# Gated layer and experts issued in a written order, low weight parts stored once and read back, logits spread over the next unit

## The chip, the cores and the metric

One Trainium2 chip, one of its cores. The metric is device time in microseconds (us) of one execution of the whole program; the kernel before has a median of 1438.2 us over three runs.

## What is computed

Three layers in one launch, all in float32. Attention with heads mixed before and after the softmax (4 batches, 12 heads, 448 positions, 64 per head) gives `x` of 1792 tokens by 768. Then a gated layer, then a layer of eight experts of which each token takes one:

```python
g = x @ w_gate                                  # 768 -> 1536
x = (g * (1.0 / (1.0 + np.exp(-g))) * (x @ w_val)) @ w_out
logits = x @ w_gate2                            # 768 -> 8
expert_idx = np.argmax(logits, axis=1)
gate_w = probs[np.arange(N), expert_idx]        # softmax of the logits
out[mask] = gate_w[mask, None] * (np.maximum(x[mask] @ w1[e], 0.0) @ w2[e])
```

## The kernel before

**Precision.** A matmul of the two layers runs as three matmuls (`mm3`, L485 to L488): every operand is split in a high part, a rounded copy, and a low part, the rest. The three products are high by high (L486), low weight by high (L487) and high weight by low (L488). So every weight tile is loaded as float32 (`wraw`, L471, 768 KB), copied on ScalarE into its high part (`whi`, L474) and subtracted into its low part (`wlo`, L476), on GpSimd for most tiles and on VectorE for those in `LOW_W`. Tiles are counted through: 0 to 17 are the gated layer's 18 tiles for the first unit, 18 to 71 the same 18 tiles three times more, 72 to 135 the experts'. In tiles 18 to 71 all low parts are made on GpSimd.

**Gated layer.** The tokens go in four units of 448. A unit has two stages. In the first, twelve tiles `ft`: 18 matmuls into the PSUM tile `pg` and 18 into `pv`; then ScalarE takes the exponential of `pg` (L618), VectorE adds 1 (L619), takes the reciprocal (L620), and multiplies by `pg` (L621) and by `pv` (L622); ScalarE and GpSimd split the product into `hhi` (L625) and `hlo` (L626). In the second, six tiles `c` of 36 matmuls over all twelve `hhi`/`hlo`; ScalarE copies each result to `x2T` (L656). The PSUM pool of these matmuls has five buffers, the pool of split weights four for each part, that of raw weights three.

**Rows, logits, routing.** After a unit, `rows` (L513) transposes `x2T` to token rows on TensorE (L520), copies them out of PSUM on VectorE and ScalarE (L522) and stores them (L524). `logits` (L526) then makes 32 dot products of rows with the experts' gate vectors on VectorE (L532, output `junk`), two to a tile of the next unit's first stage (`LGS`), and `route` (L537) picks the expert, counts each token's place in it with small matmuls (L552 to L567) and scatters token numbers and gates to a table (L584). The last unit makes half of each dot product on VectorE (L653) and the other half as matmuls (L640); the first expert's tokens are fetched (L601) by places taken from PSUM.

**Experts.** For each: 18 small transposes of fetched rows (L686), 144 + 144 matmuls of 264 columns, rectified and split on ScalarE and VectorE (L738, L739), and results transposed back (L702), scaled by the gate (L707, L709) and scattered (L711).

**Order.** Attention issues in a written order: inside `tc.manual_schedule` each engine takes its instructions as the program lists them, waits included. `feed_forward` has no such region before: a planner with its own cost estimates orders each engine's instructions, and `next_w` only says that loads and splits are traced up to three tiles ahead (`AHEAD`). Loads and stores go through SP's queue in the order in which SP gets to them; the planner places some of the gated layer's first instructions among attention's last ones.

Of the kernel before, what the change touches and what calls it, by code (L numbers as in the profile page):

```python
# [11 lines left out]
F32 = mybir.dt.float32  # L12
# [11 lines left out]
U = 448  # L24
# [20 lines left out]
LGS = [2] * 12 + [4, 4]  # L45
AHEAD = 3
# [369 lines left out]
def feed_forward(tc, xT, wf, wg, wt, w1, w2, cs, out, x2, tab, keep):  # L416
    nc = tc.nc
    V = nc.vector
    with ExitStack() as ctx:
# [3 lines left out]
        pm, pt, pr = P("pmm", 5, "p"), P("ptp", 2, "p"), P("prt", 1, "p")  # L423
        CS, NB = keep
        nc.sync.dma_start(out=CS, in_=cs)
        ID = CS[:, :128]
        IE = CS[:112, 352:384].rearrange("p (j e) -> p j e", e=NE)
        TH = CS[:112, 416:512].rearrange("p (e i) -> p e i", i=OVB)
        UO = cst.tile([112, 224], BF16, name="UO")
        V.tensor_copy(UO, CS[:112, 128:352])  # L430
        UT, ON = UO[:, :112], UO[:, 112:]
        ONF = CS[:112, 240:352]
        WG = cst.tile([128, 6, NE], F32, name="WG")
        nc.sync.dma_start(out=WG, in_=wg)
        WT = cst.tile([112, NE, DM], F32, name="WT")
        pf = cst.tile([128, NE * STR // 128, 2], I32, name="pf")
        nc.gpsimd.memset(pf[:, :, 0:1], NT)
        nc.gpsimd.memset(pf[:, :, 1:2], 0)
        nc.sync.dma_start(out=tab.rearrange("(p n) t -> p n t", p=128), in_=pf)
        zr = cst.tile([128, DM // 128], F32, name="zr")  # L440
        nc.gpsimd.memset(zr, 0.0)
        nc.sync.dma_start(out=x2[NT].rearrange("(p n) -> p n", p=128), in_=zr)
        ti = cst.tile([112, 4], I32, name="ti")
        nc.gpsimd.iota(ti, pattern=[[112, 4]], base=0, channel_multiplier=1)
        tf = cst.tile([112, 4], F32, name="tf")
        V.tensor_copy(tf, ti)
        tk = []
        for u in range(4):
            tk.append(cst.tile([112, 4], F16, name=f"tk{u}"))
            V.tensor_scalar(out=tk[u], in0=tf, scalar1=float(u * U - NT), scalar2=None, op0=ALU.add)  # L450
        iot = cst.tile([112, CAP], F16, name="iot")
        nc.gpsimd.iota(iot, pattern=[[1, CAP]], base=0, channel_multiplier=0, allow_small_or_imprecise_dtypes=True)
        first = cst.tile([TS, 3], F32, name="first")
        V.memset(first, float(NT))
        TB0 = cst.tile([TS, 3], I32, name="TB0")
        RS = cst.tile([112, NE], F32, name="RS")
        V.tensor_copy(RS, CS[:112, 384:392])

# [5 lines left out]
        ready, last, at = {}, {}, {"load": 0, "use": 0}  # L464

        def fill(n):
            while at["load"] <= min(n, len(src) - 1):
                k = at["load"]
                at["load"] += 1
                r = raw.tile([128, 12, 128], F32, name="wraw")  # L470
                last["w"] = nc.sync.dma_start(out=r, in_=src[k])  # L471
                a = wh.tile([128, 12, 128], F32R, name="whi")
                b = wh.tile([128, 12, 128], F32R, name="wlo")
                nc.scalar.copy(a, r)  # L474
                eng = nc.vector if k in LOW_W else nc.gpsimd
                eng.tensor_tensor(out=b, in0=r, in1=a.bitcast(F32), op=ALU.subtract)  # L476
                ready[k] = (a, b)

        def next_w():
# [10 lines left out]
        def order(inst, earlier):  # L490
            tc.add_manual_dep(from_inst=inst.ins, to_name=earlier.ins.name, info=mybir.DependencyInfo(mybir.DependencyClass.NoSync, mybir.DependencyReason.SCHED_ONLY))

        def apart(group, inst):
            tc.declare_no_dep(inst.ins, group=group, reason="every token has its own row")
            tc.add_to_no_dep_group(group, inst.ins)

        XS, routed = {}, []

        def load_x(u):
            XS[u] = []  # L500
            for c in range(6):
                r = xr.tile([128, U], F32, name="xraw")
                nc.sync.dma_start(out=r, in_=xT[:, c, u * U:u * U + U])
                a = xp.tile([128, U], F32R, name="xhi")
                b = xp.tile([128, U], F32R, name="xlo")
                nc.scalar.copy(a, r)
                nc.gpsimd.tensor_tensor(out=b, in0=r, in1=a.bitcast(F32), op=ALU.subtract)  # L507
                XS[u].append((a, b))
# [4 lines left out]
        def rows(u, x2T, row, halves):  # L513
            for j in range(4):
                if 0 in halves:
                    row.append(ro.tile([112, DM], F32, name="row"))
                for hf in halves:
                    t = pt.tile([128, 3, 128], F32, name="tp")
                    for i in range(3):
                        nc.tensor.transpose(t[:112, i, :], x2T[3 * hf + i][:, 112 * j:112 * j + 112], ID)  # L520
                    copy = nc.scalar.copy if hf else V.tensor_copy
                    copy(row[j][:, 384 * hf:384 * hf + 384], t[:112].rearrange("p i c -> p (i c)"))  # L522
                lo, hi = 384 * halves[0], 384 * halves[-1] + 384
                nc.sync.dma_start(out=x2[u * U + 112 * j:u * U + 112 * j + 112, lo:hi], in_=row[j][:, lo:hi])  # L524

        def logits(u, row):  # L526
            lg = T("lgs")
            done = 0
            for n in LGS:
                for j, e in [divmod(i, NE) for i in range(done, done + n)]:  # L530
                    jk = sm.tile([112, DM], F32, name="junk", bufs=1)
                    V.tensor_tensor_reduce(out=jk, in0=row[j], in1=WT[:, e, :], scale=1.0, scalar=0.0, op0=ALU.mult, op1=ALU.add, accum_out=lg[:, j, e:e + 1])  # L532
                done += n
                yield
            yield from route(u, lg)

        def route(u, lg):  # L537
# [23 lines left out]
            fi = pr.tile([112, 4, NE], F32, name="rt").rearrange("p j e -> p (j e)")[:TS, :3]  # L561
            eqs = [sm.tile([112, CAP], F16, name="at", bufs=4) for j in range(4)]
            for j in range(4):
                V.tensor_scalar(out=eqs[j], in0=iot, scalar1=sf[:, j, :], scalar2=None, op0=ALU.is_equal)
            for t in range(3):
                for j in range(4):
                    nc.tensor.matmul(fi[:, t:t + 1], eqs[j][:, t * TS:t * TS + TS], tk[u][:, j:j + 1], start=(j == 0), stop=(j == 3))  # L567
            V.tensor_tensor(out=TB0 if u == 3 else first, in0=fi, in1=first, op=ALU.add)
            if u == 3:
                fetch(0)  # L570
# [3 lines left out]
            nc.scalar.activation(ex, sh, AF.Exp)  # L574
# [3 lines left out]
            si = T("si", (112, 4), I32)  # L578
            V.tensor_copy(si, sf[:, :, 0])
            en = T("en", (112, 4, 2), I32)  # L580
            V.reciprocal(out=en[:, :, 1:2].bitcast(F32), in_=sx)
            V.tensor_scalar(out=en[:, :, 0], in0=tf, scalar1=float(u * U), scalar2=None, op0=ALU.add)
            for j in range(4):
                sc = nc.gpsimd.indirect_dma_start(out=tab, out_offset=bass.IndirectOffsetOnAxis(ap=si[:, j:j + 1], axis=0), in_=en[:, j, :], in_offset=None)  # L584
                apart("tab", sc)
                if u == 3:
                    order(sc, last["gather"])
                routed.append(sc)
            nr = T("nr", (112, NE, 1))
            V.tensor_reduce(out=nr, in_=oh.rearrange("p j e -> p e j"), axis=AX.X, op=ALU.add)  # L590
            V.tensor_tensor(out=RS, in0=RS, in1=nr[:, :, 0], op=ALU.add)

        TB = cst.tile([TS, NE, 3, 2], I32, name="TB")
        XE, RG = {}, {}

        def fetch(e):
            RG[e] = []
            for t in range(3):
                r = ro.tile([112, DM], F32, name="row")
                ap = TB[:, e, t, 0:1] if e else TB0[:, t:t + 1]  # L600
                last["gather"] = nc.gpsimd.indirect_dma_start(out=r[:TS, :], out_offset=None, in_=x2, in_offset=bass.IndirectOffsetOnAxis(ap=ap, axis=0))  # L601
                RG[e].append(r)


        fill(0)
        load_x(0)
        later = iter(())
        for u in range(4):
            hs = []
            for ft in range(12):  # L610
                w = next_w()
                pg = pm.tile([128, 512], F32, name="mm")
                pv = pm.tile([128, 512], F32, name="mm")
                for ps, o in ((pg, 0), (pv, 6)):
                    for c in range(6):
                        mm3(ps[:, :U], w, o + c, XS[u][c], c == 0, c == 5)
# [227 lines left out]
```

## Time and profile before

| | |
|---|---|
| three runs | 1437.43, 1438.2, 1438.92 us |
| profiled execution | 1438.62 us; span from first to last instruction 1436.8 us |
| mean granted TensorE clock | 0.978 of full speed |
| busy | PE 94%, PEld 82%, DVE 61%, ACT 46%, POOL 58% of the span |
| attention | to about 501 us |
| gated layer, units 0 to 3 | 501 to 637.6, to 787.3, to 937.5, to 1095.2 us |
| between gated layer and experts | 1095.2 to 1112.3 us |
| experts and end | 1112.3 to 1436.8 us |

PE is TensorE's matmuls, PEld its weight loads, DVE is VectorE, ACT ScalarE, POOL GpSimd, SP the engine that issues loads and stores. A unit's end is taken as the start of its last copy to `x2T`. Matmuls are pipelined: one of 448 columns lasts 0.36 us in the trace, and the next begins 0.20 us after it, so the number of matmuls in a stretch tells more than their busy time. The arrow in a row names what ended an idle time.

### The profile page before, as it was taken

To read this page: it belongs to the slowest core of one execution; us is meant where nothing else is said; L and a number is where in the kernel's file an instruction comes from. 1 tells how busy PE (TensorE), PEld (TensorE's weight loads), DVE (VectorE), ACT (ScalarE), POOL (GpSimd) and SP (SyncE) were. 2 spreads that over 40 slices of the span, in tenths; PEclk is the share of its full clock that TensorE was granted. 3 is DMA by queue.
4 is the path that set the end of the run, shared out by engine and by line. 5 is a ranking of instruction groups with operands and counts; after the bars stand their busy time and mean duration, and the time that the engine had idled before them with its cause. 6 is when DMAs were issued, how large, how long until landed. Compare 5 with 4: busy or idle time off the path is not lost.

```text
span 1436.8 us, 24827 instructions
## 1 busy us (share of the span) xinstructions
PE 1349.2 (94%) x9100; PEld 1174.4 (82%) x9100; DVE 874.8 (61%) x1691; ACT 661.8 (46%) x1261; POOL 835.0 (58%) x603
## 2 busy tenths in 40 slices
PE   8999999998999999999999998999986999999995
PEld 3677777776777789989889887988875999999995
DVE  3677777767767778429960998089946333333330
ACT  4675776767666533422232233232321445454551
POOL 4575566556644554735575467646643566666751
PEclk9999999999999999999999999999997999999998
DMA  7887887788786765432243323242333566666650
GB/s 244 244 256 236 232 260 242 224 260 251 223 246 208 231 206 168 139 126 98 91 134 123 127 89 110 98 143 88 110 107 108 142 221 197 216 196 209 198 174 21
DMA packets 106833, 251.23 MB, mean 175 GB/s; under 512 B 28189, under 2 KB 71293, under 8 KB 106591
## 3 DMA queue, kind: packets, MB, share of 16 engines
q1 hardware_dynamic: 102351, 237.54, 52.7%
q0 software_dynamic: 4352, 12.02, 3.0%
q8 instruction: 74, 1.21, 0.4%
q14 instruction: 56, 0.46, 0.1%
HBM read 180.00 MB, written 31.79 MB: 147 GB/s over the span
## 4 chain that ended last, share of the span: by engine, by line
PE 63%; DVE 20%; issue 6%; DMA 5%; ACT 3%; POOL 1%; SPq 1%; POOLq 0%; ACTq 0%; DVEq 0%
PE mm L488 12%; PE mm L486 12%; PE mm L487 12%; PE pso L275 8%; PE psm L247 7%; DVE e L620 7%; DVE junk L532 6%; PE psv L303 5%; PE psq L234 4%; DMA qraw<-in_qt 2%; DVE e L619 2%; DVE e L622 1%; DVE e L621 1%; PE tp L702 1%; DMA xm<-S 1%
## 5 line engine op out<-in xcount | busy, mean ns | idle before, releaser
L476 POOL TENSOR_TENSOR wlo<-wraw,whi 128x1536 fp32r<-128x1536 f32 x108 | 383.1, 3547 | 200.9 <-ACT whi L474 180.1
L486 PE MATMUL mm<-xhi,whi 128*128 128x448 f32 (+1 forms) x960 | 325.9, 340 | 11.3 <-DVE e L621 9.4
L488 PE MATMUL mm<-xlo,whi 128*128 128x448 f32 (+1 forms) x960 | 322.1, 336 | 1.4 <-POOL xlo L507 1.4
L487 PE MATMUL mm<-xhi,wlo 128*128 128x448 f32 (+1 forms) x960 | 322.0, 335 | 0.0
L474 ACT CAST whi<-wraw 128x1536 fp32r<-128x1536 f32 x136 | 200.9, 1477 | 68.1 <-PE mm L488 50.2
L486 PE MATMUL mm<-hhi,whi 128*128 128x264 f32 (+1 forms) x672 | 221.5, 330 | 7.6 <-ACT hhi L625 7.6
L488 PE MATMUL mm<-hlo,whi 128*128 128x264 f32 (+1 forms) x672 | 218.2, 325 | 1.8 <-POOL hlo L626 1.8
L487 PE MATMUL mm<-hhi,wlo 128*128 128x264 f32 (+1 forms) x672 | 217.4, 324 | 0.0
L275 PEld LDWEIGHTS pso<-kk,e 120*112 120x112 f32 x1440 | 170.5, 176 | 46.6 <-POOL kk L267 11.9
L486 PEld LDWEIGHTS mm<-xhi,whi 128*128 128x128 f32 x960 | 181.9, 190 | 24.5 <-DVE e L621 13.2
L275 PE MATMUL pso<-kk,e 120*112 120x120 f32 x1440 | 179.9, 268 | 13.6 <-ACT AT L283 7.0
L488 PEld LDWEIGHTS mm<-xlo,whi 128*128 128x128 f32 x960 | 181.7, 189 | 11.5 <-POOL xlo L507 2.1
L267 POOL TENSOR_SCALAR kk<-K,r 120x120 f32<-120x120 f32 x180 | 108.2, 602 | 140.9 <-DVE r L264 112.3
L487 PEld LDWEIGHTS mm<-xhi,wlo 128*128 128x128 f32 x960 | 182.3, 190 | 9.3 <-issue 0.2
L247 PE MATMUL psm<-xm,K 120*120 120x448 f32 x360 | 169.4, 553 | 5.8 <-DMA xm<-S 5.8
L255 ACT ACTIVATE e<-psm,nm 120x448 f32<-120x448 f32 x180 | 115.4, 641 | 98.3 <-DVE r L264 96.6
L620 DVE RECIPROCAL e<-e 128x448 f32<-128x448 f32 x48 | 141.5, 2947 | 0.7
L486 PEld LDWEIGHTS mm<-hhi,whi 128*128 128x128 f32 x672 | 128.6, 191 | 13.5 <-ACT hhi L625 8.7
L532 DVE CUSTOM_DVE_ANT_0 junk<-row,WT 112x768 f32<-112x768 f32 x96 | 135.0, 1407 | 0.9 <-ACT row L522 0.7
L488 PEld LDWEIGHTS mm<-hlo,whi 128*128 128x128 f32 x672 | 128.5, 191 | 8.3 <-POOL hlo L626 3.4
L487 PEld LDWEIGHTS mm<-hhi,wlo 128*128 128x128 f32 x672 | 128.8, 192 | 4.8
L626 POOL TENSOR_TENSOR hlo<-e,hhi 128x448 fp32r<-128x448 f32 x48 | 66.4, 1384 | 107.7 <-ACT hhi L625 107.7
(125 smaller groups left out, 2004.5 us busy)
## 6 DMA issues: line engine op xcount, KB each, us to landing
wraw<-wf SPq DMA_DIRECT2D x72, 768.0 KB
wraw<-in_w SPq DMA_DIRECT2D x64, 768.0 KB
xm<-S SPq DMA_DIRECT2D x360, 105.0 KB
f<-in_wx SPq DMA_DIRECT2D x72, 384.0 KB
wf<-cva SPq DMA_DIRECT2D x72, 192.0 KB
qraw<-in_qt SPq DMA_DIRECT2D x56, 180.0 KB
kraw<-in_kt SPq DMA_DIRECT2D x18, 448.0 KB
vt<-in_vt SPq DMA_DIRECT2D x16, 336.0 KB
```

Source lines behind the costliest of these rows:

```text
L247: nc.tensor.matmul(ps[:, :S], K1, XS.pop(n), start=True, stop=True)
L255: nc.scalar.activation(e, ps[:, :S], AF.Exp, bias=nm, scale=1.0, accum_out=su)
L267: nc.gpsimd.tensor_scalar(out=kk, in0=K2, scalar1=r2, scalar2=1.0, op0=ALU.mult, op1=ALU.mult)
L275: nc.tensor.matmul(po[:, c, :120], e[:, 112 * c:112 * c + 112], kk, start=True, stop=True)
L303: nc.tensor.matmul(pa[64 * s:64 * s + 64, j % 3, :n], VT[b][c][:, g * 64:g * 64 + 64], ATS[t][:, c, g, :n], start=(c == 0), stop=(c == 3))
L474: nc.scalar.copy(a, r)
L476: eng.tensor_tensor(out=b, in0=r, in1=a.bitcast(F32), op=ALU.subtract)
L486: nc.tensor.matmul(ps, w[0][:, j, :], x[0], start=first, stop=False)
L487: nc.tensor.matmul(ps, w[1][:, j, :], x[0], start=False, stop=False)
L488: nc.tensor.matmul(ps, w[0][:, j, :], x[1], start=False, stop=last)
L532: V.tensor_tensor_reduce(out=jk, in0=row[j], in1=WT[:, e, :], scale=1.0, scalar=0.0, op0=ALU.mult, op1=ALU.add, accum_out=lg[:, j, e:e + 1])
L620: V.reciprocal(out=e, in_=e)
```

## The change

- The whole of `feed_forward` becomes a written order on all five engines. Loads run to tile i+4 and splits to tile i+2 when tile i is taken (`take`).
- Tiles 0 to 17: the low part, once made, is stored to a DRAM tensor `wl` (`keep_low`, 18 stores of 768 KB). Tiles 18 to 71: the low part is loaded from `wl` by SP and not computed.
- The addition of 1 goes from DVE to ACT, as an activation with a bias.
- Rows of unit u are transposed, taken (both halves on ACT) and stored in the first four tiles of unit u+1; the 32 logits follow, none in tile 0, two in tiles 1 to 11, then 3, 3, 2, 2 in the second stage; `route` runs in its fourth to sixth tile.
- In the second stage the first two tiles `c` run eleven of their twelve steps, then both last ones. The next unit's `x` is split one chunk to a tile.
- The last unit's logits are all matmuls (six chunks in place of three), its first row halves are transposed in the second stage; around the routing stand ten extra matmuls (`warm`) whose results nobody reads.
- `gather(0)` stands ahead of the rest of `route`, whose table scatters follow it; a one-element memset goes to POOL with each scatter. The constants are made in tiles 1 and 4 of unit 0.

```diff
-LGS = [2] * 12 + [4, 4]
-AHEAD = 3
+LGS = [0] + [2] * 11 + [3, 3, 2, 2]
...
+        ctx.enter_context(tc.manual_schedule(engines=ORDERED))
...
+        def split(to):
+            while at["split"] <= min(to, len(src) - 1):
+                k = at["split"]
+                at["split"] += 1
+                r = rawt.pop(k)
                 a = wh.tile([128, 12, 128], F32R, name="whi")
                 b = wh.tile([128, 12, 128], F32R, name="wlo")
+                A.copy(a, r)
+                if 18 <= k < 72:
+                    nc.sync.dma_start(out=b.bitcast(F32), in_=wl[k % 18])
+                else:
+                    (V if k in LOW_W else G).tensor_tensor(out=b, in0=r, in1=a.bitcast(F32), op=ALU.subtract)
+                    if k < 18:
+                        kept.append((k, b))
                 ready[k] = (a, b)
...
+        def take():
             i = at["use"]
             at["use"] += 1
-            fill(i + AHEAD)
+            keep_low()
+            load(i + 3)
+            split(i + 2)
+            load(i + 4)
             return ready.pop(i)
...
+                if u > 0 and 1 <= ft <= 4:
+                    put_row(u - 1, ft - 1)
...
+                    if u > 0 and ft < 4:
+                        turn_row(u - 1, ft, o // 6)
                 e = ew.tile([128, U], F32, name="e")
-                nc.scalar.activation(e, pg[:, :U], AF.Exp, scale=-1.0)
-                V.tensor_scalar(out=e, in0=e, scalar1=1.0, scalar2=None, op0=ALU.add)
+                A.activation(e, pg[:, :U], AF.Exp, scale=-1.0)
+                A.activation(e, e, AF.Copy, bias=1.0)
                 V.reciprocal(out=e, in_=e)
...
+                if u > 0:
+                    for n in range(sum(LGS[:ft]), sum(LGS[:ft + 1])):
+                        logit(u - 1, n)
...
+            begin(0)
+            second(0, range(11))
+            beside(0)
+            begin(1)
+            second(1, range(11))
+            second(0, (11,))
+            end(0)
+            second(1, (11,))
+            end(1)
...
+        go = route(3)
+        warm(1)
+        chunk_logits(5)
+        next(go)
...
+        warm(2)
+        next(go)
+        fetch(0)
+        warm(6)
+        for _ in gather(0):
+            pass
+        for _ in go:
+            pass
```

## Rows read from the trace of the kernel before

**Rows 1.** Page, part 4: the chain that ended last, share of the span by engine
```profile
PE 63%; DVE 20%; issue 6%; DMA 5%; ACT 3%; POOL 1%; SPq 1%; POOLq 0%; ACTq 0%; DVEq 0%
```

**Rows 2.** Stretches: length, busy of PE, PEld, DVE, ACT, POOL, clock, DMA share, GB/s
```profile
501.00:637.60 136.60, 133.71 (x652) 122.74 (x649) 77.79 (x64) 47.67 (x56) 75.85 (x40) 0.99 0.50 160
637.60:787.30 149.70, 140.95 (x692) 126.99 (x691) 104.74 (x136) 46.28 (x59) 91.03 (x40) 0.98 0.35 114
...
937.50:1095.20 157.70, 145.28 (x713) 129.60 (x711) 128.32 (x201) 43.02 (x53) 81.42 (x33) 0.97 0.32 108
1095.20:1112.30 17.10, 6.76 (x53) 5.36 (x51) 7.94 (x29) 3.40 (x6) 9.30 (x7) 0.63 0.47 134
...
1150.00:1190.00 40.00, 40.00 (x340) 40.00 (x339) 14.24 (x21) 20.09 (x32) 26.56 (x15) 1.00 0.68 226
```

**Rows 3.** Stretches of 40 us in the first stages of units 0 and 1, same columns
```profile
560.00:600.00 40.00, 40.00 (x199) 37.09 (x198) 29.73 (x22) 15.40 (x20) 24.29 (x13) 1.00 0.35 112
...
660.00:700.00 40.00, 40.00 (x195) 36.32 (x195) 40.00 (x46) 11.83 (x14) 24.86 (x10) 1.00 0.26 89
```

**Rows 4.** Timeline of DVE, one tile of unit 1: start us, us, instruction
```profile
667.08 0.61 DVE L622 TENSOR_TENSOR e<-e,mm 128x448 f32<-128x448 f32 x1
...
668.80 2.94 DVE L620 RECIPROCAL e<-e 128x448 f32<-128x448 f32 x1
671.66 2.49 DVE L532 CUSTOM_DVE_ANT_0 junk<-row,WT 112x768 f32<-112x768 f32 x1
...
674.08 0.61 DVE L621 TENSOR_TENSOR e<-e,mm 128x448 f32<-128x448 f32 x1
674.61 0.94 DVE L532 CUSTOM_DVE_ANT_0 junk<-row,WT 112x768 f32<-112x768 f32 x1
...
675.49 0.61 DVE L622 TENSOR_TENSOR e<-e,mm 128x448 f32<-128x448 f32 x1
```

**Rows 5.** Timeline of POOL, the same tile
```profile
668.37 1.51 POOL L626 TENSOR_TENSOR hlo<-e,hhi 128x448 fp32r<-128x448 f32 x1 [3.45 <-ACT hhi L625]
669.84 3.49 POOL L476 TENSOR_TENSOR wlo<-wraw,whi 128x1536 fp32r<-128x1536 f32 x1
```

**Rows 6.** Waits of PE, 637 to 790 us: us in total, times, longest
```profile
PE mm L486 <- ACT hhi L625: 2.5, 1, 2.5
```

**Rows 7.** Groups of instructions, 560 to 1437 us: busy us, mean ns | idle before, releaser
```profile
L474 ACT CAST whi<-wraw 128x1536 fp32r<-128x1536 f32 x125 | 184.6, 1477 | 46.1 <-PE mm L488 34.6 <-issue 11.5
...
L619 DVE TENSOR_SCALAR e<-e 128x448 f32<-128x448 f32 x41 | 30.5, 745 | 13.5 <-ACT e L618 13.5
...
L625 ACT CAST hhi<-e 128x448 fp32r<-128x448 f32 x42 | 23.8, 568 | 162.6 <-DVE e L622 162.6
...
L618 ACT ACTIVATE e<-mm 128x448 f32<-128x448 f32 x41 | 22.3, 544 | 24.8 <-PE mm L488 22.7 <-POOL hlo L626 2.2
...
L567 PE MATMUL rt<-tk,at 112*88 112x1 f16 x48 | 4.5, 195 | 4.9 <-DVE at L564 4.9
...
L640 PE MATMUL mm<-WG,x2T 128*112 128x8 f32 x24 | 2.7, 237 | 0.0
```

**Rows 8.** Timeline of PE, unit 3: six transposes and the matmul behind them
```profile
1064.63 0.82 PE L520 MATMUL tp<-CS,x2T 128*112 128x128 f32 x6
1065.21 0.45 PE L486 MATMUL mm<-hhi,whi 128*128 128x448 f32 x1
```

**Rows 9.** Timeline of SP, from attention to the gated layer
```profile
486.86 0.43 SPq L471 DMA_DIRECT2D wraw<-wf  x1
...
504.25 0.56 SPq L312 DMA_DIRECT2D xT<-X  x1
```

**Rows 10.** Timeline of DVE, routing of the last unit
```profile
1097.77 2.55 DVE L543 TENSOR_TENSOR eq<-lgs,mx 112x32 f32<-112x32 f32 x1
```

**Rows 11.** DMA view, 520 to 1060 us: packets, MB, rate; the queue's share of 16 engines
```profile
DMA packets 14189, 64.12 MB, mean 119 GB/s; under 512 B 1824, under 2 KB 4128, under 8 KB 14048
...
q1 hardware_dynamic: 13904, 63.71, 35.7%
```

More of the change, by code (lines that the diff above doesn't have):

```diff
@@ L499, in load_x @@
[L499 to L508, printed above, removed]
+        XR, XS = {}, {}
@@ new lines, in load_x, with split_x @@
+        def load_x(u, c):
+            XR[u, c] = xr.tile([128, U], F32, name="xraw")
+            nc.sync.dma_start(out=XR[u, c], in_=xT[:, c, u * U:u * U + U])
+        def split_x(u, c):
+            r = XR.pop((u, c))
+            a = xp.tile([128, U], F32R, name="xhi")
+            b = xp.tile([128, U], F32R, name="xlo")
+            A.copy(a, r)
+            G.tensor_tensor(out=b, in0=r, in1=a.bitcast(F32), op=ALU.subtract)
+            XS.setdefault(u, []).append((a, b))
+        load(0)
@@ new lines, in feed_forward @@
+        for c in range(2):
+            load_x(0, c)
+        load(1)
+        split(0)
+        for c in range(6):
+            split_x(0, c)
+            if c < 4:
+                load_x(0, c + 2)
+        load(2)
+        split(1)
+        load(3)
+        WT = cst.tile([112, NE, DM], F32, name="WT")
+        WG = cst.tile([128, 6, NE], F32, name="WG")
+        UO = cst.tile([112, 224], BF16, name="UO")
+        pf = cst.tile([128, NE * STR // 128, 2], I32, name="pf")
+        ti = cst.tile([112, 4], I32, name="ti")
@@ new lines, in feed_forward @@
+        tf = cst.tile([112, 4], F32, name="tf")
+        tk = [cst.tile([112, 4], F16, name=f"tk{u}") for u in range(4)]
+        iot = cst.tile([112, CAP], F16, name="iot")
+        TB0 = cst.tile([TS, 3], I32, name="TB0")
+        first0 = cst.tile([TS, 3], F32, name="first")
+        gap = cst.tile([1, 1], F32, name="gap")
+        RS = cst.tile([112, NE], F32, name="RS")
+        ID = CS[:, :128]
+        IE = CS[:112, 352:384].rearrange("p (j e) -> p j e", e=NE)
+        TH = CS[:112, 416:512].rearrange("p (e i) -> p e i", i=OVB)
@@ L526, in logits @@
[L526 to L535, printed above, removed]
@@ L537, in route, with turn_row, take_row @@
-        def route(u, lg):
+        X2T, ROW, HALF, LG, routed, late = {}, {}, {}, {}, [], []
+        def turn_row(u, j, hf):
+            t = HALF[u, j, hf] = pt.tile([128, 3, 128], F32, name="tp")
+            for i in range(3):
+                nc.tensor.transpose(t[:112, i, :], X2T[u][3 * hf + i][:, 112 * j:112 * j + 112], ID)
+        def take_row(u, j, hf, eng=None):
+            if (u, j) not in ROW:
+                ROW[u, j] = ro.tile([112, DM], F32, name="row")
+            (eng or A.copy)(ROW[u, j][:, 384 * hf:384 * hf + 384], HALF.pop((u, j, hf))[:112].rearrange("p i c -> p (i c)"))
@@ new lines, in put_row, with logit, chunk_logits @@
+        def put_row(u, j, lo=0, hi=DM):
+            nc.sync.dma_start(out=x2[u * U + 112 * j:u * U + 112 * j + 112, lo:hi], in_=ROW[u, j][:, lo:hi])
+        def logit(u, n):
+            if n == 0:
+                LG[u] = T("lgs")
+            j, e = divmod(n, NE)
+            jk = sm.tile([112, DM], F32, name="junk", bufs=1)
+            V.tensor_tensor_reduce(out=jk, in0=ROW[u, j], in1=WT[:, e, :], scale=1.0, scalar=0.0, op0=ALU.mult, op1=ALU.add, accum_out=LG[u][:, j, e:e + 1])
+        def chunk_logits(c):
+            for j in range(4):
+                nc.tensor.matmul(LG[3][:, j, :], X2T[3][c][:, 112 * j:112 * j + 112], WG[:, c, :], start=(c == 0 and j == 0), stop=(c == 5 and j == 3))
@@ L674, in feed_forward @@
-        for t in range(3):
-            ld = nc.sync.dma_start(out=TB[:, :, t, :], in_=tab.rearrange("(e s) t -> s e t", e=NE)[t * TS:t * TS + TS])
-            for sc in routed:
-                tc.add_manual_dep(from_inst=ld.ins, to_name=sc.ins.name, info=mybir.DependencyInfo(mybir.DependencyClass.Sync, mybir.DependencyReason.DATA))
-        RT = cst.tile([112, NE, DM], F32, name="WT")
-        at["row"] = 0
         def gather(e):
@@ new lines, in feed_forward @@
+        go = route(3)
+        warm(1)
+        chunk_logits(5)
+        next(go)
+        for j in (0, 1):
+            turn_row(3, j, 1)
+        for j in (0, 1):
+            take_row(3, j, 1)
+            put_row(3, j, 384, DM)
+        warm(1)
+        next(go)
+        for j in (2, 3):
+            turn_row(3, j, 1)
+        for j in (2, 3):
+            take_row(3, j, 1)
+            put_row(3, j, 384, DM)
+        warm(2)
+        next(go)
+        fetch(0)
+        warm(6)
+        for _ in gather(0):
+            pass
@@ L694, in put @@
+        for _ in go:
+            pass
+        for t in range(3):
+            ld = nc.sync.dma_start(out=TB[:, :, t, :], in_=tab.rearrange("(e s) t -> s e t", e=NE)[t * TS:t * TS + TS])
+            for sc in routed:
+                tc.add_manual_dep(from_inst=ld.ins, to_name=sc.ins.name, info=mybir.DependencyInfo(mybir.DependencyClass.Sync, mybir.DependencyReason.DATA))
+        RT = cst.tile([112, NE, DM], F32, name="WT")
         def put(e, y):
-            first = at["row"]
+            row0 = at["row"]
@@ L698, in put @@
                 for t in range(3):
-                    row = RT[:, (first + t) % NE, :]
+                    row = RT[:, (row0 + t) % NE, :]
                     p = pt.tile([128, 3, 128], F32, name="tp")
@@ L821, in build @@
         wf = dr.tile([18, 128, 12, 128], F32, name="wf")
+        wl = dr.tile([18, 128, 12, 128], F32, name="wl")
         x2 = dr.tile([NT + 1, DM], F32, name="x2")
```

314 lines of the change are left out of this document (156 added, 158 removed).

## The prediction

> **What bounds the kernel now.** I read the chain of waits first: PE carries 63% of the span and DVE 20% [rows 1], so somewhere DVE sets the pace. The table of stretches says where [rows 2]. Unit 0 of the gated layer takes 136.6 us, unit 1 149.7, unit 3 157.7, and unit 2 what is left of the 457.6 us between 637.6 and 1095.2, 150.2. Yet the matmuls are the same 648 in each: 432 in the first stage and 216 in the second. In the experts PE is busy 40.00 of 40 us; nothing is to be had there but by doing less.
>
> What a unit costs when PE never waits comes from two stretches with PE at 40.00 of 40 us [rows 3]. Without logits beside them 199 matmuls begin in 40 us, 0.201 us each; with logits 195, 0.205 us. A first-stage tile of 36 matmuls therefore takes 7.38 us in units 1 to 3.
>
> DVE needs longer. From one multiplication by `pv` to the next is 675.49 - 667.08 = 8.41 us [rows 4]: reciprocal 2.86 (to the next start), two multiplications 0.53 each, one logit 0.88, one logit 2.42, and the rest is L619 and a further logit. The long logit runs under GpSimd's `wlo` subtraction, which holds from 669.84 for 3.49 us and ends just before that logit does [rows 5]; the same logit free of it is the 0.94 one. DVE, with the help of a blocking GpSimd, is the bound of the tiles with logits. A second, smaller loss sits between the stages: PE waits 2.5 us for the last `hhi` [rows 6].
>
> **The change, part by part.** *Low parts read back, units 1 to 3.* 54 subtractions of about 3.5 us leave POOL [rows 5]. What remains there per tile is `hlo`, 1.51 us while DVE works. It starts some 0.6 us after the multiplication by `pv` (ACT's split lies between, 0.568 us [rows 7]), so it finds the first logit running and can hold only the second. If that one stays as long as the long one was (2.42), DVE takes 2.86 + 0.53 + 0.53 + 0.88 + 2.42 = 7.2 us; with both free 2.86 + 1.06 + 1.76 = 5.7. Both are under PE's 7.38, so PE becomes the bound; I take 7.2, since `hlo` follows every product, and keep 5.7 to 8.0 for the range.
>
> *The addition moves to ACT.* DVE loses 0.745 us a tile, ACT gains what its exponential takes, 0.544 [rows 7]. ACT then has 1.48 (L474) + 0.54 + 0.54 + 0.57 = 3.1 us of the 7.38, and in four tiles two row copies. Queued behind `hhi` on ACT are the split of the weight tile, then the next exponential; the ring `hhi`, split, exponential, addition, reciprocal, two multiplications is 0.57 + 1.48 + 0.54 + 0.54 + 2.94 + 0.61 + 0.61 = 7.3 us, just under a PE tile, and 7.8 where a row copy lies in it. Those four tiles fall behind by 0.4 us each; PE has five PSUM buffers for two per tile and runs on. Cost nothing, under that cover; without it 4 x 0.4 = 1.6 us per unit.
>
> [...]
>
> *Logits spread and rows moved into the first four tiles.* The same 24 transposes per unit, behind other matmuls: six push the next matmul back by 1065.21 - 1064.63 = 0.58 us [rows 8], so 2.3 us. Routing costs PE 12 small matmuls, 4.5/4 = 1.1 us [rows 7], and six more, at the same price 0.6. The wait for the last `hhi` goes [rows 6]: twenty-two other steps stand ahead of the two that need it, 22 x 3 x 0.201 = 13 us.
>
> *Unit 3.* Logits as matmuls: 24 passes took 2.7 us [rows 7], so the 40 passes ahead of the last matmul take 4.5; twelve half-row transposes 1.2.
>
> *Sum of the units.* 432 x 0.205 + 216 x 0.201 = 132.0; with 2.3 + 1.7, 136.0 us for units 1 and 2, and 141.7 for unit 3: 413.7 against 457.6, **-43.9 us**. If PE held 0.201 with logits too, it is 5 us less.
>
> *Start.* SP now takes attention's last store, the first weight tile and the `x` chunks in the listed order, though the planner may still place the new region's first instructions among attention's last. Today the first weight load goes out at 486.86 and attention's last store at 504.25 [rows 9]. Unit 0 lies 136.6 - 648 x 0.201 = 6.4 us above its matmuls, all of it start. The second weight load now stands ahead of four `x` chunks: I take +1.5, with -3 (half of what is lost now) and +8 as ends (all loads behind 504.25). The 18 stores in unit 0 double its traffic for weights to 1.57 MB a tile; they wait on POOL, and behind them on SP stand loads that are due three tiles later, so they cost nothing.
>
> *Between gated layer and experts.* [...] L543, a 32-element comparison, took 2.55 us there [rows 10]; POOL's split no longer falls there, so some 2.3 us go. Against it, all 18 transposes of `gather(0)` now stand ahead of the first expert's matmuls, and three `warm` matmuls stand ahead of the routing's small ones. I take 0, bounds -5 (the comparison, and the clock kept up) and +5 (what two of the listed waits could add at the length of [rows 10]). The experts' table is loaded later, since its scatters follow `gather(0)`, and every weight load behind it on SP waits with it; four of an expert's eight tiles are in by then, about 20 us of PE work (288 matmuls and 36 transposes an expert, 340 instructions in 40 us [rows 2]), so nothing. POOL's memsets beside the scatters, and its fetch for the second expert two steps later, fall in POOL's idle third [rows 2].
>
> *Experts.* PE is full before and has the same instructions after [rows 2]: 0, as long as the written order keeps splits two tiles ahead.
>
> **Sum.** -43.9 + 1.5 + 0 = -42.4. The profiled execution took 1438.62 us, 0.4 above the median of the runs; 1438.62 - 42.4 = 1396.2, and against the median 1395.8. I say **1396 us**.
>
> **Rivals.** *DVE or the ACT ring still bounds.* For it: 7.2 and 7.3 us leave 0.1 to 0.2 us a tile. Against it: PE needs DVE only two tiles later. At 8.0 us a tile 33 x 0.62 = 20 us come back: 1416 us. [...]
>
> *Read-back makes DMA the bound, slower than before.* A tile of units 1 to 3 loads 2 x 0.786 MB, and `x` and rows (448 x 768 x 4 bytes each) add 2.8 MB a unit, 0.155 a tile: 1.73 MB in 7.38 us, 234 GB/s. It decides where the queue falls under this; to end 2.9 us (0.2%) above today the 54 tiles must take (42.4 + 2.9)/54 = 0.84 us more each, 8.2 us, 210 GB/s, and then 1441 us or more. For it: the gated layer moves only 119 GB/s now [rows 11]. Against it: that took 35.7% of the engines, 333 GB/s at full share, and the experts moved 226 at 0.68 [rows 2].
>
> *The written order does not reach into attention.* If the planner does not mesh the two regions, the early loads of today are lost and the start costs 8 in place of 1.5: 1402.5 us. Nothing in the trace excludes it, but today's early load [rows 9] comes from the same planner.
>
> **How the numbers follow.** Forecast 0.70, ring or DVE 0.12, start 0.12, DMA 0.06. The range reaches down by the faster matmuls (5), the start (4.5) and the gap (5): 1396 - 14.5, say 1382; up to the ring rival, 1416. What a measurement of this kernel can tell from no change is 0.2%, about 3 us. Slower is the DMA rival, 0.06; the same needs two rivals at once, 0.03; faster 0.91.
>
> **What would show it.** Units 1 and 2 at 136 us and unit 3 near 142, PE at 40.00 of 40 us in their first stages, DVE idle for a little in each tile, L532 with one long and one short in each pair, no L476 on POOL between tiles 18 and 71, a DMA rate near 234 GB/s at a share near 0.7. Wrong it is if `wlo` loads end PE's waits (DMA), if the exponentials end a row of PE waits on `pg` (ring), if the first L486 comes after 508 us (start), or if PE waits in the experts behind the later table.

## The result, and the profile after

| | before | after |
|---|---|---|
| median (lowest to highest), us | 1438.56 (1437.43 to 1438.92) | 1425.47 (1423.07 to 1431.59) |
| ratio, 95% interval | | 0.9912 (0.9891 to 0.9933) |
| profiled execution; its span | 1438.62; 1436.8 | 1431.59; 1429.7 |

The change gains 0.9%, 13 us of the 42 forecast; 1425.47 lies above the range. The profiled execution of after is the slowest of its four runs, so between the two profiles there are 7.1 us.

Where they went is read from marks in the timelines: the last copy to `x2T` of each unit and the first `hhi` of each expert.

| us | before | after | after less before |
|---|---|---|---|
| end of unit 0 | 637.6 | 642.2 | +4.6 |
| units 1 to 3 | 457.6 | 416.2 (137.3, 137.0, 141.9) | -41.4 |
| to the first expert's `hhi` | 23.6 | 24.0 | +0.4 |
| from there to the end | 317.9 | 347.2 | +29.3 |

The units lost what was forecast. The experts, forecast at nothing, took 29 us back.

The stretches of after (columns as in [rows 2]): unit 0, units 1 and 3, the gap, the first expert, 40 us of the second.

```profile
503.70:642.20 138.50, 136.15 (x648) 122.16 (x647) 62.80 (x51) 52.56 (x69) 67.44 (x38) 0.99 0.79 278
642.20:779.50 137.30, 137.30 (x691) 124.75 (x691) 94.55 (x120) 53.48 (x75) 24.34 (x24) 1.00 0.64 227
916.50:1058.40 141.90, 141.90 (x743) 129.92 (x743) 95.93 (x120) 52.42 (x73) 24.68 (x20) 1.00 0.58 193
1058.40:1082.50 24.10, 18.62 (x96) 13.04 (x96) 7.81 (x28) 5.73 (x13) 6.19 (x10) 0.79 0.23 64
1082.50:1136.00 53.50, 41.58 (x321) 40.73 (x320) 12.95 (x23) 18.56 (x30) 25.97 (x15) 0.87 0.48 148
1145.00:1185.00 40.00, 40.00 (x339) 39.90 (x338) 14.27 (x21) 19.89 (x32) 27.40 (x16) 1.00 0.61 196
```

In units 1 and 3 PE is busy for the whole stretch (against [rows 2]); in unit 1 POOL falls from 91 to 24 us, and DMA runs at 227 GB/s and a share of 0.64. In the first expert PE stands still for 12 of 53.5 us and its granted clock is 0.87 in the mean; that expert took 36.8 us before.

DVE in one tile of unit 1 (compare [rows 4]), then POOL's only instruction beside it (compare [rows 5]), then ACT:

```profile
687.34 2.95 DVE L681 RECIPROCAL e<-e 128x448 f32<-128x448 f32 x1 [0.42 <-ACT e L680]
...
691.05 0.62 DVE L683 TENSOR_TENSOR e<-e,mm 128x448 f32<-128x448 f32 x1
691.59 0.95 DVE L571 CUSTOM_DVE_ANT_0 junk<-row,WT 112x768 f32<-112x768 f32 x1
...
692.59 1.79 DVE L571 CUSTOM_DVE_ANT_0 junk<-row,WT 112x768 f32<-112x768 f32 x1
...
698.52 0.62 DVE L683 TENSOR_TENSOR e<-e,mm 128x448 f32<-128x448 f32 x1
```

```profile
692.35 1.21 POOL L689 TENSOR_TENSOR hlo<-e,hhi 128x448 fp32r<-128x448 f32 x1 [6.25 <-ACT hhi L688]
```

```profile
692.18 1.48 ACT L447 CAST whi<-wraw 128x1536 fp32r<-128x1536 f32 x1
693.56 0.53 ACT L679 ACTIVATE e<-mm 128x448 f32<-128x448 f32 x1
694.12 0.58 ACT L680 ACTIVATE e<-e 128x448 f32<-128x448 f32 x1
```

From one product with `pv` to the next is 698.52 - 691.05 = 7.47 us; PE's own tiles take 7.44 there, by the starts of their matmuls. DVE idles 0.42 us before the reciprocal, for ACT's addition, and on ACT the exponential and the addition follow the split without a pause. So the ring of the prediction has no slack in this tile: it falls 0.03 us a tile behind PE, which has buffers for that. The long logit, 1.79 us against 0.95 of the one before it, starts while `hlo` runs, and `hlo` ends 0.82 us before it does.

The view of [rows 6], waits of PE in unit 1 of before (us in total, times, longest), names three more:

```profile
PE tp L520 <- DVE row L522: 2.8, 1, 2.8
PE mm L486 <- DVE e L621: 2.4, 2, 1.6
PE mm L488 <- POOL hlo L626: 1.0, 1, 1.0
```

With the 2.5 us of [rows 6] they make 8.7 of the 12.4 us that unit 1 lost; the other 3.7, by estimate, go with the lower granted clock (0.98 against 1.00: 2% of 149.7 us is 3.0). In units 1 to 3 of after the view names no wait. From 1080 us to the end of after it names:

```profile
PE tp L648 <- DMA row<-x,TB: 14.4, 8, 5.3
PE mm L474 <- POOL wlo L451: 4.3, 3, 2.9
```

The way there begins on POOL and SP. Below, POOL around the first expert; then the waits of SP in 1060 to 1110 us; then PE.

```profile
1080.95 0.97 POOL L628 DMA_INDIRECT tab<-en,si  x1 [10.23 <-DVE en L626]
...
1085.51 0.94 POOL L628 DMA_INDIRECT tab<-en,si  x1 [0.22 <-issue]
...
1097.55 3.44 POOL L451 TENSOR_TENSOR wlo<-wraw,whi 128x1536 fp32r<-128x1536 f32 x1 [7.47 <-ACT whi L447]
1101.18 2.33 POOL L640 DMA_INDIRECT row<-x,TB  x1 [0.19 <-issue]
...
1105.12 0.98 POOL L640 DMA_INDIRECT row<-x,TB  x1 [0.30 <-issue]
```

```profile
SPq L793 <- DMA tab<-en,si: 25.7, 1, 25.7
```

```profile
1101.05 0.39 PE L474 MATMUL mm<-hhi,wlo 128*128 128x264 f32 x1 [2.95 <-POOL wlo L451]
1109.43 0.38 PE L648 MATMUL tp<-CS,row 88*128 88x88 f32 x1 [5.33 <-DMA row<-x,TB]
1112.83 0.41 PE L648 MATMUL tp<-CS,row 88*128 88x88 f32 x1 [3.01 <-DMA row<-x,TB]
```

The table's scatters (L628) stand behind `gather(0)` and end at 1086.5. SP waits 25.7 us for them with the table's load, and every weight load stands behind that: ACT's split has its next raw weights at 1095.99, POOL its subtraction at 1097.55, and behind the subtraction POOL issues the second expert's fetch (L640) at 1101.18. Its rows come some 8 us later. One late transfer goes through four in-order queues, SP, ACT, POOL and PE.

### The profile page after: what moved, and what is told of

The parts are those of the page before. It is cut to its first block, busy times and chain, and to the rows that moved or that the text cites. A ratio compares the mean times of both kernels' runs of the same rounds, so it can differ in the third digit from the quotient of the medians.

```text
span 1429.7 us, 24918 instructions
## 1 busy us (share of the span) xinstructions
PE 1357.1 (95%) x9144; PEld 1179.4 (82%) x9144; DVE 810.1 (57%) x1562; ACT 690.2 (48%) x1325; POOL 636.4 (45%) x589
## 4 chain that ended last, share of the span: by engine, by line
PE 74%; DMA 10%; issue 5%; POOL 5%; ACT 2%; SPq 2%; DVE 1%; POOLq 0%; ACTq 0%; DVEq 0%
PE mm L473 16%; PE mm L475 16%; PE mm L474 16%; PE pso L274 8%; PE psm L246 7%; PE psv L302 4%; PE psq L233 4%; DMA qraw<-in_qt 2%; DMA row<-x,TB 2%; POOL wlo L451 2%; DMA xm<-S 2%; DMA wraw<-in_w 2%; POOL row L640 1%; SPq L241 1%; PE tp L648 1%
## 5 line engine op out<-in xcount | busy, mean ns | idle before, releaser
L451 POOL TENSOR_TENSOR wlo<-wraw,whi 128x1536 fp32r<-128x1536 f32 x54 | 189.3, 3508 | 135.8 <-ACT whi L447 135.0
L681 DVE RECIPROCAL e<-e 128x448 f32<-128x448 f32 x48 | 141.7, 2952 | 97.8 <-ACT e L680 97.8
L474 PEld LDWEIGHTS mm<-xhi,wlo 128*128 128x128 f32 x960 | 182.1, 190 | 10.1
L689 POOL TENSOR_TENSOR hlo<-e,hhi 128x448 fp32r<-128x448 f32 x48 | 57.2, 1191 | 292.5 <-ACT hhi L688 292.5
L688 ACT CAST hhi<-e 128x448 fp32r<-128x448 f32 x48 | 27.3, 568 | 213.9 <-DVE e L683 213.9
```

The lines of the kernel that those rows point to most:

```text
L451: (V if k in LOW_W else G).tensor_tensor(out=b, in0=r, in1=a.bitcast(F32), op=ALU.subtract)
L474: nc.tensor.matmul(ps, w[1][:, j, :], x[0], start=False, stop=False)
L681: V.reciprocal(out=e, in_=e)
L689: G.tensor_tensor(out=hl, in0=e, in1=hh.bitcast(F32), op=ALU.subtract)
```

## The experiments

Every median stands beside runs of the kernel before on the same chip (1438.66, 1438.37 and 1438.98 us in the three batches).

**e1_scatter_first: the scatters ahead of `gather(0)`.**

```diff
         fetch(0)
+        for _ in go:
+            pass
         warm(6)
         for _ in gather(0):
             pass
-        for _ in go:
-            pass
```

> Theory (the table's loads hold SP): in the changed kernel the scatters of the last unit's routing run after all of gather(0), so the table loads on SP wait until 1089.5 us and weight tile 76 behind them lands only near 1096; the fetch of the second expert's rows stands on POOL behind that tile's subtraction. With the scatters ahead of gather(0) the first expert (first hhi to the second expert's first hhi, 53.5 us changed, 36.8 before) takes 38 to 41 us, and the median is 1410 to 1414 us against 1425 changed. Rival (the first expert is slow because its fetch goes out late in the written order of POOL, whatever the table does): 49 us or more, median over 1420.

Measured: 1414.82 us, ratio 0.9832 (0.9800 to 0.9863); the first expert takes 46.3 us (53.5 in after), between the two expectations. The late table is 7 us of that expert's loss and not all of it. PE still waits 9.9 us for rows over all experts.

**e2_fetch_early: an expert's rows fetched one expert ahead.** The first fetch stays.

```diff
-                if f == (5 if e == 0 else 3) and e + 1 < NE:
-                    fetch(e + 1)
+                if f == 5 and e == 0:
+                    fetch(1)
...
+                if c == 4 and e + 2 < NE:
+                    fetch(e + 2)
```

> Only the fetches for experts 2 to 7 are issued earlier, in the second stage of the expert two before. Theory (later experts wait for rows fetched too late): experts 1 to 6 take 38.4 us each as before, where two of them took 41.3 and 44.4; 9 to 11 us less than changed, median 1414 to 1417. Rival (those waits come from weight subtractions on POOL that are late, not from the fetch): no more than 3 us less, 1422 to 1426.

Measured: 1415.53 us, ratio 0.9834 (0.9807 to 0.9860). Experts two to seven take 38.3 to 38.4 us, as before; the first still 53.0. In after they took 38.5, 41.3, 39.3, 38.5, 44.4 and 39.3, because the fetch stands on POOL behind scatters and a subtraction. POOL in the third expert of after, up to the first fetch of the fourth expert's rows; then a fetch of the fourth expert's rows in before (timelines):

```profile
1179.83 3.54 POOL L451 TENSOR_TENSOR wlo<-wraw,whi 128x1536 fp32r<-128x1536 f32 x1
1183.56 1.00 POOL L816 DMA_INDIRECT out<-WT,TB  x1 [0.19 <-issue]
...
1184.86 1.55 POOL L640 DMA_INDIRECT row<-x,TB  x1 [0.22 <-issue]
```

```profile
1185.47 1.01 POOL L601 DMA_INDIRECT row<-x,TB  x1 [3.59 <-PE tp L686]
```

In before the planner issued this one 27.5 us ahead of the first transpose of that expert's rows (1213.01). In after the first is issued 8.9 us ahead (1193.73), and the three waits around that transpose come to 2.3 us. The margin is narrow: the fetches of the third, fifth, sixth and eighth expert, 10.1 us ahead, cost PE no wait; that of the seventh, 9.5 us ahead, cost 3.1 us.

**e3_both: both edits.**

> Both edits. If the two losses are separate, they add: 22 to 27 us less than changed, median 1398 to 1404 us, about what I forecast for the change itself (1396), the rest being the start. If one hides the other, 1408 to 1414.

Measured: 1406.39 us, ratio 0.9769 (0.9742 to 0.9795), 2 us above the range; 19.1 us less than after, where the two edits alone gave 10.7 and 9.9. The first expert still takes 45.3 us: its own fetch of the second expert's rows is issued at 1093.69, behind two subtractions, and PE waits 5.2 us for it.

**e6_fetch_one_early: e3_both, and the second expert's rows fetched in step 1.**

```diff
-                if f == 5 and e == 0:
+                if f == 1 and e == 0:
                     fetch(1)
```

> Both earlier edits, and the second expert's rows fetched at step 1 of the first expert in place of step 5. In the run with both edits PE waited 5.4 us for these rows and the first expert took 45.3 us; their fetch stood on POOL behind the subtraction of tile 75 or 76 and went out at 1093.7, 12 us after the first hhi. If its place in POOL's list is the cause, the first expert takes 37 to 39 us and the median falls by 6 to 8, to 1398 to 1401 us. Rival (the table arrives too late for it): over 43 us, median 1404 or more, and POOL waits for the table with weight subtractions behind it.

Measured: 1400.76 us, ratio 0.9732 (0.9703 to 0.9761). First expert 37.5 us, the others 38.3 to 38.4. All that PE waits for from 1080 us on:

```profile
PE tp L807 <- DVE WT L814: 0.3, 1, 0.3
```

So three moves in the written order, with no byte or instruction less, give back 24.7 us (1425.47 - 1400.76): nearly the whole of the experts' loss.

**e5_gated_only: the written order ends with the scatters, the planner orders the experts.**

```diff
-        ctx.enter_context(tc.manual_schedule(engines=ORDERED))
+        region = ctx.enter_context(ExitStack())
+        region.enter_context(tc.manual_schedule(engines=ORDERED))
...
+        region.close()
```

> The written order ends with the table scatters; the table's loads and the experts go back to the planner. Theory (the written order is what costs in the experts, because a wait there holds everything listed behind it on its queue): units 1 to 3 stay at 416 us, the first expert takes 37 to 39 us in place of 53.5, the others 38.4, median 1396 to 1402 us. Rival (the loss comes from the late scatters alone, whoever orders the rest): first expert 45 us or more, median 1405 or more.

Measured: 1412.45 us, ratio 0.9824 (0.9807 to 0.9842), with a first expert of 45.5 us, a gap of 28.6 and experts of 38.3 to 38.4 after that. The planner mends the later experts and not the first, whose table is still late: the rival's numbers. But the late scatters alone are not the cause either: with them early and the fetch late (e3) the first expert takes 45.3 us, and only with both early (e6) 37.5.

**e4_planner_readback: the kernel before with the read-back alone.** Planner, logits, rows and the addition as before.

```diff
...
-                eng = nc.vector if k in LOW_W else nc.gpsimd
-                eng.tensor_tensor(out=b, in0=r, in1=a.bitcast(F32), op=ALU.subtract)
+                if 18 <= k < 72:
+                    nc.sync.dma_start(out=b.bitcast(F32), in_=wl[k % 18])
+                else:
+                    eng = nc.vector if k in LOW_W else nc.gpsimd
+                    eng.tensor_tensor(out=b, in0=r, in1=a.bitcast(F32), op=ALU.subtract)
+                    if k < 18:
+                        nc.sync.dma_start(out=wl[k], in_=b.bitcast(F32))
...
```

> The kernel before with the read-back alone: no written order, the addition on DVE, logits where they were. Theory (GpSimd's subtractions blocking DVE were the bound of the tiles with logits): units 1 to 3 fall from 457.6 to 420 to 435 us, experts stay at the 318 us of before, median 1412 to 1422 us. Rival (the written order is what shortened the units): units 1 to 3 above 450 us, median 1432 or more. If the planner orders the stores badly, unit 0 grows over 140 us.

Measured: 1400.72 us, ratio 0.9741 (0.9710 to 0.9771). Units 1 to 3 take 416.6 us (135.4, 135.4, 145.9), unit 0 ends at 638.3, the experts are those of before: a larger gain than I expected. The read-back alone brings what the whole change brings in the units, and loses nothing elsewhere. Units 1 and 3 (columns as in [rows 2]), then the logits of units 1 to 3 (busy us, mean ns; before had 135.0 and 1407):

```profile
638.30:773.70 135.40, 135.40 (x692) 124.75 (x691) 87.80 (x136) 47.06 (x60) 27.49 (x22) 1.00 0.69 230
909.05:1055.00 145.95, 141.90 (x714) 127.83 (x712) 109.29 (x202) 43.86 (x53) 29.38 (x18) 0.99 0.58 192
```

```profile
L537 DVE CUSTOM_DVE_ANT_0 junk<-row,WT 112x768 f32<-112x768 f32 x96 | 91.8, 957 | 0.9 <-ACT row L527 0.7
```

With the subtractions gone, the same 96 logits take 43.2 us less.

**e7_no_readback: the changed kernel with every low part computed.**

```diff
-                if 18 <= k < 72:
-                    nc.sync.dma_start(out=b.bitcast(F32), in_=wl[k % 18])
-                else:
-                    (V if k in LOW_W else G).tensor_tensor(out=b, in0=r, in1=a.bitcast(F32), op=ALU.subtract)
-                    if k < 18:
-                        kept.append((k, b))
+                (V if k in LOW_W else G).tensor_tensor(out=b, in0=r, in1=a.bitcast(F32), op=ALU.subtract)
```

> The changed kernel with all low parts computed, none stored or read back. Theory (subtractions of 3.5 us on GpSimd hold two-input instructions of DVE): a tile with two logits takes 7.7 to 8.1 us again, units 1 to 3 take 426 to 436 us in place of 416, median 1434 to 1445 us. Rival (the written order and the addition on ACT had made room enough): units 1 to 3 under 420, median 1424 to 1429.

Measured: 1430.06 us, ratio 0.9939 (0.9915 to 0.9963); units 1 to 3 take 422.0 us. Inside the written order, with the addition on ACT, the read-back is worth 5.8 us only: between the two expectations, nearer the rival's. In the first stage the subtraction runs beside the reciprocal, which it does not lengthen (2.95 us), and not beside the logits (0.95 and 1.79 us, as in after), and a tile stays at 7.47 us. In the second stage logits beside a subtraction take up to 4.15 us, and in units 1 and 2 PE waits 1.7 us each for the routing behind them.

**e8_add_on_dve: the changed kernel with the addition back on DVE.**

```diff
-                A.activation(e, e, AF.Copy, bias=1.0)
+                V.tensor_scalar(out=e, in0=e, scalar1=1.0, scalar2=None, op0=ALU.add)
```

> The changed kernel with the addition of 1 on DVE again. DVE now sits idle 0.4 to 1.3 us a tile for ACT, so I expect no difference that can be told: units 1 to 3 within 3 us of 416, median 1423 to 1428. Rival (DVE was only just below PE's tile, as my sum had it): 33 tiles times 0.3 to 0.6 us, units 1 to 3 at 426 to 436, median 1434 or more. [...]

Measured: 1449.0 us, ratio 1.0070 (1.0046 to 1.0093), slower than before. Neither side fits: units 1 to 3 take 415.9 us, no more than in after, and yet the median is beyond the rival's. The loss is in unit 0, which ends at 655.5 us; in the kernels with the written start and the addition on ACT it ends at 635.6 to 642.2. In unit 0 the low parts are still computed. DVE and POOL there (timelines):

```profile
539.77 0.39 DVE L680 TENSOR_SCALAR e<-e 128x448 f32<-128x448 f32 x1
...
546.98 3.30 DVE L680 TENSOR_SCALAR e<-e 128x448 f32<-128x448 f32 x1 [1.69 <-ACT e L679]
550.31 2.95 DVE L681 RECIPROCAL e<-e 128x448 f32<-128x448 f32 x1
```

```profile
546.58 3.45 POOL L451 TENSOR_TENSOR wlo<-wraw,whi 128x1536 fp32r<-128x1536 f32 x1 [0.23 <-ACT whi L447]
556.76 3.48 POOL L451 TENSOR_TENSOR wlo<-wraw,whi 128x1536 fp32r<-128x1536 f32 x1 [0.28 <-ACT whi L447]
```

The addition of 0.39 us that starts just after a subtraction lasts until the subtraction is done, and the written order brings them together in eight of unit 0's twelve tiles (3.30 to 4.30 us; 0.38 or 0.39 in the other four, whose low part DVE makes): `hhi`, the next split and the next exponential follow each other on ACT, and they release the subtraction and the addition within half a microsecond. PE waits 11.2 us for `wlo` in this unit.

**e9_planner_add_act: the kernel before with the addition alone on ACT.**

```diff
-                V.tensor_scalar(out=e, in0=e, scalar1=1.0, scalar2=None, op0=ALU.add)
+                nc.scalar.activation(e, e, AF.Copy, bias=1.0)
```

> The kernel before, under its planner, with only the addition of one moved from VectorE to ScalarE; every low part is still computed. Theory (VectorE's cycle bounds the units of before, and the addition is in it with 0.38 us alone and 1.34 us and more where GpSimd's subtraction of a low part runs beside it): some 0.75 us a tile go, 36 tiles, so units 1 to 3 take 425 to 440 us instead of 457.6, and the median is 1405 to 1425 us. Rival (the long logits of 2.49 us alone hold the units, or the planner puts something else beside the subtractions): units over 450 us, median within 5 us of before.

Measured: 1439.49 us, ratio 1.0007 (0.9991 to 1.0024); units 1 to 3 take 457.5 us. My expectation failed, the rival is right. Groups of units 1 to 3 (busy us, mean ns), first of before, then of this kernel:

```profile
L532 DVE CUSTOM_DVE_ANT_0 junk<-row,WT 112x768 f32<-112x768 f32 x96 | 135.0, 1407 | 0.9 <-ACT row L522 0.7
...
L619 DVE TENSOR_SCALAR e<-e 128x448 f32<-128x448 f32 x36 | 25.1, 698 | 7.5 <-ACT e L618 7.5
```

```profile
L532 DVE CUSTOM_DVE_ANT_0 junk<-row,WT 112x768 f32<-112x768 f32 x96 | 141.6, 1475 | 1.3 <-ACT row L522 0.7
L620 DVE RECIPROCAL e<-e 128x448 f32<-128x448 f32 x36 | 106.0, 2946 | 18.1 <-ACT e L619 18.1
```

DVE lost 25.1 us of additions; the logits became 6.6 us longer and DVE idled 18.1 us for ACT's addition in place of 7.5 for its exponential. That accounts for 17.2 of the 25.1; where the other 8 went I did not trace.

**e10_planner_both: e4_planner_readback with the addition on ACT.** To the diff of e4_planner_readback comes this line.

```diff
-                V.tensor_scalar(out=e, in0=e, scalar1=1.0, scalar2=None, op0=ALU.add)
+                nc.scalar.activation(e, e, AF.Copy, bias=1.0)
```

> The kernel before, under its planner, with the read-back of the low parts (as in e4_planner_readback) and the addition on ScalarE. Theory (with the read-back units 1 and 2 already run at TensorE's pace, 135.4 us each, and the addition collides with nothing any more): units 1 to 3 take 413 to 417 us, unit 0 gains nothing, median 1397 to 1402 us, within 3 us of e4_planner_readback. Rival (unit 0, where the low parts are still computed, is held by the same collision under the planner too): unit 0 shorter by 3 us or more, median 1390 to 1396.

Measured: 1400.64 us, ratio 0.9723 (0.9693 to 0.9753): the same as e4_planner_readback, as expected. Unit 0 gains nothing. In its profiled execution units 1 to 3 took 423.4 us, more than expected; its matmuls are slower there than those of e4 (last section).

**e11_order_only: the changed kernel with the low parts computed and the addition on DVE.** The two edits of e7_no_readback and e8_add_on_dve, the second of which is

```diff
-                A.activation(e, e, AF.Copy, bias=1.0)
+                V.tensor_scalar(out=e, in0=e, scalar1=1.0, scalar2=None, op0=ALU.add)
```

> The written order alone: the changed kernel with every low part computed and the addition on VectorE. Theory (in the written order the addition starts while GpSimd subtracts a low part and is held to its end, 3.3 us for 0.39, as in unit 0 of e8_add_on_dve, whose unit 0 took 13 us longer; with the low parts computed, that comes back in all four units): units 1 to 3 take 450 us or more in all, median 1470 to 1490 us, slower than before. Rival (unit 0 of e8_add_on_dve was longer for its own start, and the spread logits leave room): units 1 to 3 take 416 to 430 us, median 1448 to 1460.

Measured: 1557.1 us, ratio 1.0826 (1.0806 to 1.0845); units 1 to 3 take 524.2 us. The theory's direction, at more than its price (450 us or more in the units, 1490 us at most). Groups of units 1 to 3:

```profile
L448 POOL TENSOR_TENSOR wlo<-wraw,whi 128x1536 fp32r<-128x1536 f32 x54 | 206.5, 3826 | 50.3 <-ACT whi L447 50.3
L566 DVE CUSTOM_DVE_ANT_0 junk<-row,WT 112x768 f32<-112x768 f32 x96 | 172.0, 1791 | 2.2
...
L675 DVE TENSOR_SCALAR e<-e 128x448 f32<-128x448 f32 x36 | 123.7, 3436 | 46.6 <-ACT e L674 45.5
```

All 36 additions are blocked, 1.5 to 3.65 us each, 3.44 on average, and from product to product a tile takes 10.6 us. On ACT the next split stands behind `hhi`, which waits for the product, and POOL's subtraction waits for the split; so PE waits for the low part (waits of PE in units 1 to 3):

```profile
PE mm L469 <- POOL wlo L448: 47.6, 21, 3.4
PE rt L589 <- DVE oh L584: 19.4, 3, 9.3
```

The logits of the first stage are as in after (0.95 and 1.79 us). Those of the second stage fall beside subtractions, take up to 4.25 us and raise the mean to 1.79 (1.26 in after); the second wait is for the routing behind them.

Units 1 to 3 together, in profiled executions:

| us | all low parts computed | and addition on ACT | low parts read back | both |
|---|---|---|---|---|
| planner's order | 457.6 (before) | 457.5 (e9) | 416.6 (e4) | 423.4 (e10) |
| written order | 524.2 (e11) | 422.0 (e7) | 415.9 (e8) | 416.2 (after) |

The large steps of the table have one cause: VectorE instructions that wait for a subtraction on GpSimd (a logit takes 1.41 us in the mean in before and 0.96 in e4, an addition 3.44 in e11 and 0.40 in e8). The read-back removes the subtraction in either order. The addition on ACT helps only in the written order, where, with the addition gone from DVE, the subtraction falls beside the reciprocal (e7). The terms do not add. The 423.4 of e10 is slower matmuls and no collision (PE waits 4.0 us in these units there, 4.1 in e4).

## Why the prediction was wrong

- **Units 1 to 3: right.** 136, 136 and 141.7 forecast, 137.3, 137.0 and 141.9 measured, in sum 2.5 us off. The logits came as worked out in kind (one of each pair blocked by `hlo`), 1.79 and not 2.42 us long. Which part of the bundle has the gain, the forecast left open: the read-back alone has it (e4). One term fitted by luck: 0.205 us a matmul "with logits". Without logits unit 0 ran at either pace, here in after and then in e1, whose program is the same up to there; e4 had logits beside it and began 200 in 40 us:

```profile
560.00:600.00 40.00, 40.00 (x195) 36.34 (x194) 24.32 (x18) 16.26 (x23) 17.61 (x10) 1.00 0.60 212
560.00:600.00 40.00, 40.00 (x199) 37.04 (x198) 24.73 (x18) 14.82 (x20) 19.83 (x9) 1.00 0.59 209
660.00:700.00 40.00, 40.00 (x200) 37.06 (x198) 39.51 (x58) 13.68 (x18) 9.07 (x6) 1.00 0.62 211
```

- **The addition on ACT.** It was put at nothing, and in units 1 to 3 it is that: with the read-back the addition takes 0.39 us on DVE (e8) and 0.58 on ACT (after), so where nothing collides DVE is the faster engine, and those units take 415.9 and 416.2 us. On DVE it costs 13 to 20 us in unit 0 (e8), where the prediction did not look: beside a subtraction the addition lasts 3.30 us against 0.39.
- **Start: within its bounds, but the +1.5 is not shown.** +4.6 us in the profile of after, with +1.5 taken and -3 to +8 as ends. The other kernels with the written start and the addition on ACT end unit 0 between 635.6 and 641.4 us, which is -2 to +4; programs that are the same up to there differ by that much. The ground for +1.5 was a misreading: the load at 486.86 of [rows 9] is the second of before (the first goes out at 482.12), and four `x` chunks stand behind it there too. The stores of the low parts cost nothing (e4: unit 0 ends at 638.3, before 637.6).
- **Gap: right, in part by luck.** +0.4 against 0; the comparison of [rows 10] takes 0.19 us in after and the first fetched rows are transposed 13.0 us after the unit instead of 17.1; with all 18 transposes ahead of the first `hhi`, that is given back. Only 2.3 of these 4.1 us were priced. The lower bound also counted on "the clock kept up"; no run shows what that is worth. In the gap the mean granted clock was 0.63 before ([rows 2]) and 0.79 after.
- **The table loaded later: here it failed.** It was put at nothing on two grounds. The first, "four of an expert's eight tiles are in by then, about 20 us of PE work", nearly held: PE waits 2.95 us for the fifth tile's `wlo`. The second, that the fetch for the second expert would "fall in POOL's idle third", is the step that failed. POOL is as idle as forecast (27.4 us busy of 40, 26.6 before), but it takes its list in order: the last split before the stop was at 1085.03, the next at 1095.99, behind that stood the subtraction and behind it the fetch, and PE waited 5.3 and 3.0 us for the rows. The prediction's closing part named PE waits behind the later table as a sign of error, but gave them no price and no rival. This is 16.7 us in the first expert; e1, e3 and e6 take it away in steps, 46.3, 45.3 and 37.5 us.
- **"Experts: 0, as long as the written order keeps splits two tiles ahead": failed too.** It looked at weights and PE's work, and the fetch of rows was what came late: 11 us in experts two to seven, all of it gone when the fetch is issued an expert ahead (e2). The last expert took 1.6 us more; that was not traced.
- **Rivals.** DMA was no bound: 227 GB/s at a share of 0.64 in unit 1, near the forecast 234. The ring and DVE did not hold PE, which has no wait in units 1 to 3, but the ring came out at 7.47 us and not 7.3, without slack.

With the two failed steps mended (e6) the written order ends at 1400.76 us, 4.8 above the forecast. The fastest versions are e4, e6 and e10, equal within their intervals, and e4 needs none of the written order.

## What to carry to other kernels

When an order is written by hand, price for each queue what stands behind every instruction that can wait, DMA issues first: a gather whose issue slips from 27.5 to 8.9 us ahead of its use costs nothing in any engine's busy time and appears as waits on another (here PE, 2.3 us). Before bundling a change, ask which part removes the collision; here one part, removing GpSimd's subtractions, had the whole gain. An instruction moved to another engine to escape a collision gains only if the first engine does not wait for it there and nothing else takes its place in the collision (e9: 10.6 us more idle time, 6.6 us longer logits).

## What was not expected of the hardware

- The addition, with one input, was held beside a GpSimd subtraction as the logits are, with two: 0.39 us alone and mostly 3.3 to 3.65 us beside it (e8, e11), a logit 0.95 and up to 4.25 us (e11). The reciprocal, with one input too, kept its 2.95 us beside such a subtraction (e7; 2.94 in [rows 4, 5]).
- Units 1 and 2 without any PE wait at a granted clock of 1.00 took 135.4 us in e4 and 137.6 in e10, with the same 692 PE instructions recorded in unit 1. Both paces, 199 or 200 and 195 in 40 us, occur at that clock, with logits and without, and in unit 0 of one and the same program (after and e1, above). What slows the matmuls is open; no run was made for it.
- A gap in PE's work cost more than its length: in the first expert of after PE stood still 12 us and the expert took 16.7 us longer than before. The granted clock was 1.00 from 1082.5 to 1105 us, 0.68 from 1105 to 1109 us, in PE's wait for the rows, and 0.50 from 1109 to 1120 us, though PE worked again from 1113. From 1118 to 1120 us, at 0.50, 11 PE instructions began, in the next 2 us, at 0.97, 20.
